# Packed attention and SwiGLU on one core: float32 second products in the first two units, GpSimd in place of a copy by DMA, and a new set of planner constants

## The chip, the core and the metric

The kernel runs on one core of a Trainium2 chip. The metric is device time in microseconds; lower is better. Three runs of the kernel before took 787.19, 790.18 and 791.77 us (median 790.18).

## The reference, cut to what matters

```python
def sm_attn(qq, kk, vv):                      # per batch and head
    s = scale * qq @ kk.T
    a = exp(s - max(s)); a = a / (sum(a) + 1e-9)
    return a @ vv
packed = sm_attn(p, k, v)                     # 32 packed rows read 576 keys
out    = sm_attn(q, packed, packed)           # 576 queries read the 32 packed rows
x = out as [4608 tokens, 512]                 # 8 batches x 576, 8 heads x 64
xn = x / sqrt(mean(x*x) + 1e-6) * rms_g
y = (silu(xn @ w_gate) * (xn @ w_val)) @ w_out     # 512 -> 1536 -> 512
```

The inputs q, k, v and p are float32. The three weight matrices arrive as float64, 1 MB for each of 18 pieces, and are made into float32 on the chip.

## The kernel before

The 4608 tokens are 12 units of 384 tokens, three tiles of 128 tokens each. A batch has 576 tokens, so units 1, 4, 7 and 10 hold tokens of two batches ("mixed" units). For each of the 8 batches `keysets` loads and transposes the keys, `stage1` makes the packed rows (32 per head), and `packed_weights` multiplies the packed rows by the gate and value weights (L1203) into a `ring` of eight slots: instead of forming x and multiplying it by the weights, the MLP multiplies the attention weights by these products. For each unit `query` brings the queries, `attention` makes the scores (L1405 or L1412), the softmax, the transposed weights `aT` and from them the second product (L1475), which is only needed for the RMS norm: ScalarE squares and sums it (L1483). The scaled weights, transposed again, are `aTu`. `mlp` then runs 24 groups of six matmuls per unit (L1593, two for each of 12 feature tiles `ft`), `gated` turns two of them into `hall` (silu L1644, product L1647, a high float16 part L1664 or L1667, a low part L1670 or L1673), and three groups of 36 matmuls (L1629, "second MLP products") make 128 output rows each, which `store` evicts.

Most products are made from float16 high and low parts, three matmuls for one. Batches and units below `EARLY = 2` take another way: their scores are float32 matmuls and their transposes go through TensorE (`transposed`, L1280) instead of a DMA. Their second product is before made like all others, of three float16 parts: `transposed` writes the high part by ScalarE (L1305) and the low part by VectorE (L1307), and `stage1` splits the packed rows `pk` into `pav` (L1163, by `split`, L452 and L454).

The weights: `gv_piece` (12 pieces of w_gate and w_val) and `wo_piece` (6 pieces of w_out) load float64 into a raw room and call `to_f32`, which uses ScalarE (L487), then GpSimd (L492) and VectorE (L494), or VectorE alone (L497, L499), as the letters of `LOW` and `LOW_WO` say. The raw rooms lie in tiles that are not in use yet: rooms 0 to 3 in `ring`, 4 to 6 in `wo`, 7 and 8 in `hall`. `RAW_AT` and `WO_AT` give each piece its room; a piece waits until the piece before it in its room is converted, loads are issued in turn, and in unit 0 the writes to `hall` wait for room 7 (`ft` up to 5) and room 8 (`ft` from 5 on). After each value piece `gv_piece` makes three scale columns `gv_sc` by four VectorE steps of one element per partition (L599, L600, L601, L607). When all six w_out pieces are there, `wo_scale` makes one scale from them, and `wo_split` writes each piece's high part by ScalarE into a spare tile (L687), its low part by VectorE in place (L689), and copies the high part to its place in `wo` by a DMA on SyncE's queue (L691). The second MLP products of unit 0 wait for these pieces, two `ft` each.

The order of all this is fixed when the kernel is built. Each function is a generator that yields steps (engine, estimated cost), and `Plan.run` plays them through a model of the engines and writes the instructions in that order into each engine's queue; the engines then run their queues in order and wait for semaphores. `RANK` and `LATER` say which chain goes first, `CHOICE` how far past the earliest possible start (in estimated us) a step of better rank may still be taken first on an engine, separately for stage 0 (until unit 1's `aTu` is planned) and stage 1, and `SLACK` adds 0.317 or 0.223 us to the start of a TensorE step that is not the MLP's. `Plan.fill` puts short matmuls of no use (L1717) into long planned gaps of TensorE.

```python
            window = CHOICE[self.stage][e]
            chain = min(
                (s for s in starts if ENGINE[s[2].ask[0]] == e and s[0] <= first[0] + window), key=lambda s: (s[1], s[0])
            )[2]
```

## Time and profile before

| | |
|---|---|
| median of three runs | 790.18 us |
| the profiled execution | 790.56 us, its span 788.4 us |
| TensorE busy (matmuls) | 748.3 us, 95% of the span |
| VectorE, ScalarE, GpSimd busy | 495.6, 465.3, 46.8 us |
| mean granted TensorE clock | 0.985 |

The span runs from the first to the last instruction; the profiled execution's own time is 2.2 us longer. A profile line gives an engine (PE is TensorE's matmuls, PEld its weight loads, DVE VectorE, ACT ScalarE, POOL GpSimd, SPq SyncE's queue of DMAs), a source line of the kernel, the tile written and the tiles read, and times. The chain of waits follows the work that ended last back from the end; in it "issue" is time in which the engine waited for nothing that the profile shows.

### The profile page before, as it was taken

The page shows a single profiled execution, that of the slowest core. Times are in us where ns is not written, and L with a number is a line of the kernel's source. Part 1 is how long each engine was busy: PE and PEld are TensorE (multiplying, and loading weights), DVE is VectorE, ACT ScalarE, POOL GpSimd, SP SyncE. Part 2 cuts the span into 40 slices and gives each one's busy share as a digit, 9 for nine tenths or more (in the row PEclk, how much of TensorE's full clock was granted, in tenths as well). Part 3 has the DMA queues.
Part 4 walks back from the last instruction along what each step waited for, and adds up shares of the span by engine and source line. Part 5 has one row for each costly group of instructions (what it writes and reads, how often), then busy time and mean ns, then how long its engine had stood idle before and what let it go on. Part 6 is the DMA issues. An engine that isn't in the chain of part 4 may idle for free.

```text
span 788.4 us, 18226 instructions
## 1 busy us (share of the span) xinstructions
PE 748.3 (95%) x7664; PEld 435.8 (55%) x7664; DVE 495.6 (63%) x1086; ACT 465.3 (59%) x884; POOL 46.8 (6%) x52
## 2 busy tenths in 40 slices
PE   8767997999999999999999999999999999999998
PEld 6533563676445555586455455586455455685553
DVE  1799986685496485568476674668476655472341
ACT  3778986576486576387377656287376455271230
POOL 1443101010000000000000000000000000000000
PEclk9989998999999999999999999999999999999999
DMA  9999234444637636714843470614613212301001
GB/s 254 387 300 250 113 94 109 90 88 109 125 78 136 138 64 132 150 43 79 170 98 65 102 157 8 151 42 91 157 36 60 69 35 61 90 13 34 27 1 41
DMA packets 137138, 83.76 MB, mean 106 GB/s; under 512 B 98528, under 2 KB 124640, under 8 KB 137056
## 3 DMA queue, kind: packets, MB, share of 16 engines
q1 hardware_dynamic: 137056, 82.59, 43.7%
q8 instruction: 60, 0.98, 0.5%
q14 instruction: 22, 0.18, 0.1%
HBM read 47.97 MB, written 9.44 MB: 73 GB/s over the span
## 4 chain that ended last, share of the span: by engine, by line
PE 72%; DVE 7%; ACT 5%; issue 3%; DMA 2%; SPq 0%; DVEq 0%; ACTq 0%
PE pm_2x L1629 9%; PE pm_1x L1629 9%; PE pm_0x L1629 9%; PE pm_0x L1593 8%; PE pm_2x L1593 7%; PE pm_1x L1593 7%; PE pm_3x L1629 6%; PE pm_3x L1593 6%; PE pm_3x L1203 1%; PE quad L1412 1%; PE quad L1052 1%; DVE ring L454 1%; PE pm_2x L1203 1%; PE quad L1475 1%; DVE t_0x L1647 1%
## 5 line engine op out<-in xcount | busy, mean ns | idle before, releaser
L1593 PEld LDWEIGHTS <-ring 128*128 128x128 f16 x2304 | 206.2, 98 | 106.9 <-issue 36.1
L1629 PEld LDWEIGHTS <-hall 128*128 128x128 f16 x1296 | 124.3, 99 | 157.1 <-issue 18.0
L1629 PE MATMUL pm_1x<-wo,hall 128*128 128x512 f16 x396 | 90.2, 382 | 0.0
L1629 PE MATMUL pm_2x<-wo,hall 128*128 128x512 f16 x324 | 73.9, 379 | 0.7 <-issue 0.7
L1629 PE MATMUL pm_0x<-wo,hall 128*128 128x512 f16 x324 | 73.4, 379 | 0.0
L1667 ACT CAST hall<-t_1x 128x384 f16<-128x384 f32 x72 | 36.8, 511 | 42.3 <-DVE t_1x L1647 42.2
L1667 ACT CAST hall<-t_0x 128x384 f16<-128x384 f32 x70 | 35.7, 510 | 36.5 <-DVE t_0x L1647 35.8
L1629 PE MATMUL pm_3x<-wo,hall 128*128 128x512 f16 x252 | 57.2, 382 | 0.0
L1673 DVE TENSOR_TENSOR hall<-t_1x,hall 128x384 f16<-128x384 f32 x70 | 38.9, 556 | 20.6 <-ACT hall L1667 19.1
L1593 PE MATMUL pm_0x<-aTu_0x,ring 128*128 128x192 f16 (+1 forms) x360 | 50.4, 283 | 1.5 <-ACT t_1x L1644 1.0
L1673 DVE TENSOR_TENSOR hall<-t_0x,hall 128x384 f16<-128x384 f32 x67 | 37.1, 554 | 16.7 <-ACT hall L1667 16.3
L1593 PE MATMUL pm_2x<-aTu_1x,ring 128*128 128x192 f16 (+1 forms) x300 | 43.3, 288 | 0.5 <-ACT t_0x L1644 0.4
L1593 PE MATMUL pm_0x<-aTu_1x,ring 128*128 128x192 f16 (+1 forms) x300 | 42.7, 286 | 0.4 <-DVE t_0x L1647 0.2
L1593 PE MATMUL pm_1x<-aTu_1x,ring 128*128 128x192 f16 (+1 forms) x300 | 42.4, 284 | 0.7 <-ACT t_0x L1644 0.7
L1593 PE MATMUL pm_1x<-aTu_0x,ring 128*128 128x384 f16 (+1 forms) x264 | 40.1, 293 | 0.5 <-DVE ring L454 0.2
L1593 PE MATMUL pm_2x<-aTu_0x,ring 128*128 128x192 f16 (+1 forms) x288 | 40.1, 283 | 0.0
L1593 PE MATMUL pm_3x<-aTu_1x,ring 128*128 128x384 f16 (+1 forms) x252 | 38.4, 294 | 1.5 <-issue 1.5
L1593 PE MATMUL pm_3x<-aTu_0x,ring 128*128 128x384 f16 (+1 forms) x240 | 35.3, 291 | 0.3 <-DVE ring L454 0.3
L454 DVE SCALAR_TENSOR_TENSOR ring<-pm_3x,pw_sc,ring 128x512 f16<-128x512 f32 x31 | 23.1, 744 | 3.8 <-ACT ring L452 3.7
L1483 ACT ACTIVATE quad<-quad 128x512 f32<-128x512 f32 x36 | 21.0, 584 | 6.0 <-PE quad L1475 5.8
L452 ACT ACTIVATE ring<-pm_3x,pw_sc 128x512 f16<-128x512 f32 x31 | 21.1, 681 | 4.6 <-PE pm_1x L1203 4.0
L454 DVE SCALAR_TENSOR_TENSOR ring<-pm_1x,pw_sc,ring 128x512 f16<-128x512 f32 x24 | 17.9, 747 | 7.4 <-ACT ring L452 7.0
(868 smaller groups left out, 1246.4 us busy)
## 6 DMA issues: line engine op xcount, KB each, us to landing
out_dram<-o_0x SPq DMA_DIRECT2D x18, 256.0 KB, 2.1
out_dram<-o_1x SPq DMA_DIRECT2D x18, 256.0 KB, 2.0
hall<-in_moe_w_out_dram SPq DMA_DIRECT2D x4, 1024.0 KB, 8.4
big_3x<-in_k_dram SPq DMA_DIRECT2D x7, 576.0 KB, 6.3
big_4x<-in_k_dram SPq DMA_DIRECT2D x6, 576.0 KB, 6.4
big_3x<-in_v_dram SPq DMA_DIRECT2D x6, 576.0 KB, 5.7
wo<-in_moe_w_gate_dram SPq DMA_DIRECT2D x3, 1024.0 KB, 15.2
wo<-in_moe_w_val_dram SPq DMA_DIRECT2D x3, 1024.0 KB, 13.0
```

What stands on the lines that cost most here:

```text
L452: nc.scalar.activation(hi, x, AF.Copy, scale=s)
L454: nc.vector.scalar_tensor_tensor(lo, x, s, hi, ALU.mult, ALU.subtract)
L1052: nc.tensor.matmul(pp[32 * j : 32 * j + 32, :D], a1T[:, c, 32 * j : 32 * j + 32], vf[:, j, cv, :], start=(c == 0), stop=(c == NCK - 1),)
L1203: nc.tensor.matmul(ps[e][32 * j : 32 * j + 32, :], pg[h, j, :], wgv[h, c, j, :, :].rearrange("p w f -> p (w f)"), start=True, stop=True,)
L1412: nc.tensor.matmul(ps2[o : o + n, i, :, pi, :], qT[:, lq, i, pi, o : o + n], packs[b][3][:, lp, pi, :, :], start=(j == 0), stop=(j == 2),)
L1475: nc.tensor.matmul(px[o : o + n, j, i, g, :], aT[h, i, la, g, o : o + n], packs[b][2][g][h, lp, :], start=(n3 == 0), stop=(n3 == 2), tile_ ...
L1483: nc.scalar.activation(x, x, AF.Square, scale=2.0**-14, accum_out=ss[:, i : i + 1])
L1593: nc.tensor.matmul(psi[:, :, o : o + n], pw[:, g, lw, w, f * P : (f + 1) * P], aT[:, :, la, g, o : o + n], start=(j == 0), stop=(j == 5),)
L1629: nc.tensor.matmul(po, hall[:, ft, lh, ts], wo[:, ft, 1 - lw, :], start=(n == 0), stop=(n == 3 * NFT - 1))
L1647: nc.vector.scalar_tensor_tensor(hall32[:, ft, :] if full else t, pss[1][:, :UT], sc[:, c, 2:3] if full else sc[:, c, 1:2], t, ALU.mult, A ...
L1667: nc.scalar.copy(hall[:, ft, 0, :], t)
L1673: nc.vector.tensor_tensor(hall[:, ft, 1, :], t, hall[:, ft, 0, :], ALU.subtract)
```

## The change

In units 0 and 1 the second product is made by float32 matmuls, one where there were three: `transposed` with `whole=True` writes `aT` as float32, two thirds by ScalarE and one third by VectorE, the packed rows are read as they are from `pks`, their scale `sv` goes into the square (`svs`, `svu`), batch 0's `pav` parts are no longer made, the unit waits for "normed" instead of "packed", and the four `pk` rooms are kept until unit 1's second product. The high parts of w_out go to their place by GpSimd (`WO_HI`, one of six by ScalarE) instead of a DMA. Three of the four `gv_sc` steps move from VectorE to GpSimd and the fourth is gone. Constants change: `WO_AT` (the raw rooms of w_out), letters that move single steps between engines, the planner's ranks, windows, latencies and step costs. `PW32` and `H32` stay off, and `PW16_FROM` stays at 8, so that all eight batches multiply by float32 weights.

```diff
--- before.py
+++ after.py
@@ -31,13 +31,13 @@
     mybir.EngineType.SP,
 )
-LATENCY = {PE: 0.299, ACT: 0.16, EXP: 0.16, SILU: 0.16, DVE: 0.14, POOL: 0.006}
+LATENCY = {PE: 0.299, ACT: 0.16, EXP: 0.16, SILU: 0.16, DVE: 0.14, POOL: 0.005}
 SLACK = (0.317, 0.223)
-CHOICE = ({'pe': 0.0, 'act': 0.458, 'dve': 0.275, 'pool': 0.298, 'sp': 0.833}, {'pe': 0.0, 'act': 0.382, 'dve': 0.13, 'pool': 0.269, 'sp': 0.274})
+CHOICE = ({'pe': 0.1, 'act': 0.458, 'dve': 0.275, 'pool': 0.298, 'sp': 0.833}, {'pe': 0.2, 'act': 0.382, 'dve': 0.13, 'pool': 0.2, 'sp': 0.274})
 IN_TURN = range(18)
 FILL = (0.9, 1.0, 400.0, 0.6)
@@ -56,8 +56,8 @@
-ACT_COST = (0.081, 0.87e-3)
-DVE_COST = (0.068, 0.953e-3)
+ACT_COST = (0.093, 0.87e-3)
+DVE_COST = (0.074, 0.953e-3)
 def act(n):
@@ -234,19 +234,19 @@
-RANK = ({"mlp": 1e9, "scales": 0, "gated": 0, "pw_evict": 0.63, "store": 0, "attention": 0.16, "stage1": 0.84, "keys": 0.18, "v": 0, "query": 0.3, "pw": 0.44, "g": 1.01, "w": 1.45, "wo": 1.05, "wo_split": 1.49, "conv": 2.38}, ...
-LATER = {"attention": -0.78, "stage1": -0.4, "keys": 0.45, "query": 0.4, "pw": -0.46, "w": 0.34, "wo": 0.0, "wo_split": 0.02}
+RANK = ({"mlp": 1e9, "scales": 0, "gated": 0.24, "pw_evict": 0.63, "store": 0, "attention": 0, "stage1": 0.84, "keys": 0, "v": 0, "query": 0.61, "pw": 0.44, "g": 0.77, "w": 1.34, "wo": 1.05, "wo_split": 1.49, "conv": 2.38}, ...
+LATER = {"attention": -0.92, "stage1": -0.4, "keys": 0.45, "query": 0.4, "pw": -0.46, "w": 0.34, "wo": 0.0, "wo_split": 0.02}
 RAW_AT = (0, 1, 2, 3, 4, 5, 6, 7, 8, 4, 5, 6)
-WO_AT = (7, 3, 8, 7, 3, 8)
+WO_AT = (8, 3, 7, 8, 3, 8)
 EARLY_ROOMS = (5, 4, 3)
 KT_IN_W = Q0_IN_W = True
 A1_ROOMS = 2
 A1T_BY = "AAAADAAA"
 VAL_BY = "DDPADD"
-LOW = "PPPPPPPPPPPP"
+LOW = "PPPPPPPPPDPP"
 LOW_WO = "PPPDDP"
 NORM_BY = "AAGAAAAAAAAA"
@@ -254,14 +254,14 @@
 KEYS_AFTER = 12
 KEYS_BY = "ADAAAAADAADA"
 QUERY_BY = "AADADA"
-H_HI = "AAAADAAAAADA"
-H_LO = "DDDPPDDDDDDP"
-H_LO_MIXED = "DDDDPDDDDDDD"
+H_HI = "AAAADAAAADDA"
+H_LO = "DPDDPDDDDDPP"
+H_LO_MIXED = "DDDDDDDDDDDD"
 H_LO_ONE = "DDDDDDDDDDDD"
-NORM_SLACK = (1.152, 3.0)
+NORM_SLACK = (1.416, 1.977)
 PW16_FROM = 8
@@ -274,10 +274,14 @@
 H32 = False
 PW32 = False
-PW_BY = "ADADADADADAD"
+PW_BY = "ADADADADDDAD"
 A1D_FROM = 8
 A1S_BY = "PPPPPPPPPPPPPPPP"
+GV_BY = "PPPPPP"
+WO_HI = "PPAPPP"
 @with_exitstack
@@ -361,7 +365,8 @@
     wo = wo32.bitcast(F16).rearrange("p f (l n) -> p f l n", l=2)
-    gv_sc = cpool.tile([P, NFC, 3], F32, name="gv_sc")
+    NSC = 3 if H32 else 2
+    gv_sc = cpool.tile([P, NFC, NSC], F32, name="gv_sc")
     pw_sc = cpool.tile([P, NFC], F32, name="pw_sc")
     wo_sc = cpool.tile([P, NFC], F32, name="wo_sc")
     wo_ss = cpool.tile([P, NFC], F32, name="wo_ss")
@@ -412,7 +417,7 @@
     rooms("tiny", 96, [P, 2], F32)
     rooms("trio", 8, [P, 3], F32)
     rooms("t24", 4, [P, 24], F32)
-    rooms("usc", 2, [P, NFC, 3], F32)
+    rooms("usc", 2, [P, NFC, NSC], F32)
     rooms("ru2", 2, [P, TPU], F32)
     if PW32:
@@ -595,16 +600,13 @@
             yield POOL, 2.9
             nc.gpsimd.tensor_scalar_mul(x, x, mx[:, 0:1])
         plan.mark("pw_sc", c)
-        yield DVE, 0.5, t0
-        nc.vector.tensor_scalar(gv_sc[:, c, 0:1], u[:, 0:1], gmax, 2.0**-5, ALU.mult, ALU.mult)
-        nc.vector.tensor_scalar(gv_sc[:, c, 1:2], s[:, 0:1], gmax_r, 2.0**-12, ALU.mult, ALU.mult)
-        nc.vector.tensor_scalar(wo_sc[:, c : c + 1], u[:, 0:1], u[:, 1:2], gsq, ALU.mult, ALU.mult)
+        by = nc.gpsimd if GV_BY[c] == "P" else nc.vector
+        yield POOL if GV_BY[c] == "P" else DVE, 0.6, t0
+        by.tensor_scalar(gv_sc[:, c, 0:1], u[:, 0:1], gmax, 2.0**-5, ALU.mult, ALU.mult)
+        by.tensor_scalar(gv_sc[:, c, 1:2], s[:, 0:1], gmax_r, 2.0**-12, ALU.mult, ALU.mult)
+        by.tensor_scalar(wo_sc[:, c : c + 1], u[:, 0:1], u[:, 1:2], gsq, ALU.mult, ALU.mult)
         if H32:
-            nc.vector.tensor_scalar(
-                gv_sc[:, c, 2:3], gv_sc[:, c, 1:2], wo_sc[:, c : c + 1], 2.0**-8, ALU.mult, ALU.mult
-            )
-        else:
-            nc.vector.tensor_copy(gv_sc[:, c, 2:3], gv_sc[:, c, 1:2])
+            by.tensor_scalar(gv_sc[:, c, 2:3], gv_sc[:, c, 1:2], wo_sc[:, c : c + 1], 2.0**-8, ALU.mult, ALU.mult)
         plan.mark("gv_sc", c)
         if PW32:
             plan.mark("sc", 0, c)
@@ -687,8 +689,12 @@
         nc.scalar.activation(hi, x, AF.Copy, scale=sc)
         yield DVE, dve(1024)
         nc.vector.scalar_tensor_tensor(wo[:, 2 * i : 2 * i + 2, 0, :], x, sc, hi, ALU.mult, ALU.subtract)
-        yield LOAD, P * 2048
-        nc.sync.dma_start(wo[:, 2 * i : 2 * i + 2, 1, :], hi)
+        if WO_HI[i] == "P":
+            yield POOL, 1.2
+            nc.gpsimd.tensor_copy(wo[:, 2 * i : 2 * i + 2, 1, :], hi)
+        else:
+            yield ACT, act(1024)
+            nc.scalar.copy(wo[:, 2 * i : 2 * i + 2, 1, :], hi)
         plan.give("o", hi0)
         plan.mark("wo_hl", i)
@@ -1110,13 +1116,14 @@
         for g in range(2):
             nc.tensor.matmul(pn, ones, ss[:, g : g + 1], start=(g == 0), stop=(g == 1))
         yield DVE, 0.8
-        uv, sv, eps = uvs[b], tiny(), epss[b]
+        uv, sv, eps = uvs[b], svs[b] if early else tiny(), epss[b]
         norm_scale(uv, sv, pn)
         if early:
...
         yield DVE, 0.2
         nc.vector.tensor_scalar(eps, sv, sv, 1e-6 * 2.0**-20, ALU.mult, ALU.mult)
+        plan.mark("normed", b)
         if not early:
             yield ACT, act(128), max(t_s, t_t)
             nc.scalar.activation(pts, ptx, AF.Copy, scale=sv)
@@ -1153,19 +1160,21 @@
             yield from split(pg[:, 0], pg[:, 1], pg32, 1.0, 128)
             plan.give("pg", pg32)
         pav = []
-        packs[b] = (uv, eps, pav, pbd, pg)
+        packs[b] = (uv, eps, pav, pbd, pg, pks)
         plan.mark("pg", b)
         plan.now = t_b
         plan.mark("pb", b)
-        for g in range(2):
+        for g in range(2) if (b + 1) * S > EARLY * UT else ():
             hl = yield Room("pav")
             yield from split(hl[:, 0], hl[:, 1], pks[g], sv, D, t_s)
-            plan.give("pk", pks[g])
+            if not early:
+                plan.give("pk", pks[g])
             pav.append(hl)
         plan.mark("packed", b)
     uvs = [cpool.tile([P, 1], F32, name=f"uv{b}") for b in range(B)]
+    svs = [cpool.tile([P, 1], F32, name=f"sv{b}") for b in range(EARLY)]
     epss = [cpool.tile([P, 1], F32, name=f"eps{b}") for b in range(B)]
@@ -1270,7 +1279,7 @@
         n = min(P, (S - r) // TPU)
         return [(b, r, 0, n)] + ([(b + 1, 0, n, P - n)] if n < P else [])
-    def transposed(dst, x, s, give, u=None):
+    def transposed(dst, x, s, give, u=None, whole=False):
         psc = yield Room("psc")
         ps = psc.rearrange("p a b -> p (a b)")[:, : TPU * HR]
@@ -1283,15 +1292,15 @@
         if give:
             plan.give("e", x)
         ps = ps.rearrange("p (i x) -> p i x", i=TPU)
-        if PW32 and u == 0:
-            x = whole(dst)
+        if whole or PW32 and u == 0:
+            x = whole32(dst)
             t0, ends = plan.now, []
             yield ACT, act(512), t0
-            nc.scalar.activation(x[:, :2], ps[:, :2].rearrange("p i (g t) -> p i g t", g=2), AF.Copy, scale=2.0)
+            nc.scalar.activation(x[:, :2], ps[:, :2].rearrange("p i (g t) -> p i g t", g=2), AF.Copy, scale=s)
             ends.append(plan.now)
             yield DVE, dve(256), t0
-            nc.vector.tensor_scalar_mul(x[:, 2], ps[:, 2].rearrange("p (g t) -> p g t", g=2), 2.0)
+            nc.vector.tensor_scalar_mul(x[:, 2], ps[:, 2].rearrange("p (g t) -> p g t", g=2), s)
             plan.now = max(ends + [plan.now])
             plan.give("psc", psc)
             return
@@ -1307,7 +1316,7 @@
         nc.vector.scalar_tensor_tensor(lo, ps, s, hi, ALU.mult, ALU.subtract)
         plan.give("psc", psc)
-    def whole(aT):
+    def whole32(aT):
         return aT.rearrange("p i l g t -> p (i l g t)").bitcast(F32).rearrange("p (i g t) -> p i g t", i=TPU, g=2)
@@ -1438,7 +1447,7 @@
             plan.give("t24", x)
         aT = yield Room("aT")
         if early:
-            yield from transposed(aT, e, 2.0**14, False)
+            yield from transposed(aT, e, 1.0, False, whole=True)
         else:
             ehl = yield Room("hl")
             yield ACT, act(768)
@@ -1453,11 +1462,16 @@
         t_a = plan.now
         for b, r, o, n in parts(u):
-            yield ("packed", b)
+            yield ("normed" if early else "packed", b)
+        svu = svs[parts(u)[0][0]] if early else None
         if len(parts(u)) > 1:
+            if early:
+                svu = tiny()
             yield DVE, 0.3
             for b, r, o, n in parts(u):
                 nc.vector.tensor_copy(eps[o : o + n], epss[b][o : o + n])
+                if early:
+                    nc.vector.tensor_copy(svu[o : o + n], svs[b][o : o + n])
         ss = trio()
         t_x = []
@@ -1468,6 +1482,15 @@
         yield PE, pe(D, 6 * TPU) + 0.4, t_a
         for i in range(TPU):
             for g in range(2):
+                if early:
+                    for j in range(4):
+                        h = slice(32 * j, 32 * j + 32)
+                        for b, r, o, n in parts(u):
+                            nc.tensor.matmul(
+                                px[o : o + n, j, i, g, :], whole32(aT)[h, i, g, o : o + n], packs[b][5][g][h, :],
+                                start=True, stop=True, tile_position=(32 * j, o),
+                            )
+                    continue
                 for n3, (la, lp) in enumerate(((0, 0), (0, 1), (1, 0))):
                     for j in range(4):
                         h = slice(32 * j, 32 * j + 32)
@@ -1480,11 +1503,15 @@
         for i in range(TPU):
             yield ACT, act(512) + 0.2, t
             x = px[:, :, i].rearrange("s j g d -> s j (g d)")
-            nc.scalar.activation(x, x, AF.Square, scale=2.0**-14, accum_out=ss[:, i : i + 1])
+            nc.scalar.activation(x, x, AF.Square, scale=svu if early else 2.0**-14, accum_out=ss[:, i : i + 1])
             t_x.append(plan.now)
         for name, room in held:
             plan.give(name, room)
         plan.give("aT", aT)
+        if u == EARLY - 1:
+            for b in range(EARLY):
+                for x in packs[b][5]:
+                    plan.give("pk", x)
         if u * UT // S != (u + 1) * UT // S:
             b = u * UT // S
@@ -1536,7 +1563,7 @@
             yield ACT, 3 * act(256), t_r
             for i in range(TPU):
                 nc.scalar.activation(e[:, i], e[:, i], AF.Copy, scale=rr[:, i : i + 1])
-            yield from transposed(aTu, e, 1.0, True, u)
+            yield from transposed(aTu, e, 2.0 if PW32 and u == 0 else 1.0, True, u)
         else:
             ahl = yield Room("hl")
             for i in range(TPU):
@@ -1580,7 +1607,7 @@
                         pw = ring[:, slot_of(b, c)]
                         if PW32 and b == 0:
                             pw = pw.rearrange("p e l w f -> p e (l w f)").bitcast(F32)
-                            x = aths[0] if u else whole(aT)
+                            x = aths[0] if u else whole32(aT)
                             for g in range(2):
                                 nc.tensor.matmul(
                                     psi[:, :, o : o + n], pw[:, g, 2 * P * w + f * P : 2 * P * w + (f + 1) * P], x[:, :, g, :],
```

More of the change, by code (lines that the diff above doesn't have):

```diff
@@ L233, in run @@
             self.go(chain)
-RANK = ({"mlp": 1e9, "scales": 0, "gated": 0, "pw_evict": 0.63, "store": 0, "attention": 0.16, "stage1": 0.84, "keys": 0.18, "v": 0, "query": 0.3, "pw": 0.44, "g": 1.01, "w": 1.45, "wo": 1.05, "wo_split": 1.49, "conv": 2.38}, {"mlp": 1e9, "scales": 0.03, "gated": 0, "pw_evict": 0, "store": 0.25, "attention": 1.21, "stage1": 0.58, "keys": 0.27, "v": 0.78, "query": 0.42, "pw": 1.83, "g": 2.14, "w": 0.92, "wo": 2.54, "wo_split": 0.63, "conv": 2.76})
-LATER = {"attention": -0.78, "stage1": -0.4, "keys": 0.45, "query": 0.4, "pw": -0.46, "w": 0.34, "wo": 0.0, "wo_split": 0.02}
+RANK = ({"mlp": 1e9, "scales": 0, "gated": 0.24, "pw_evict": 0.63, "store": 0, "attention": 0, "stage1": 0.84, "keys": 0, "v": 0, "query": 0.61, "pw": 0.44, "g": 0.77, "w": 1.34, "wo": 1.05, "wo_split": 1.49, "conv": 2.38}, {"mlp": 1e9, "scales": 0.03, "gated": 0, "pw_evict": 0, "store": 0.25, "attention": 1.21, "stage1": 0.58, "keys": 0.27, "v": 0.78, "query": 0.42, "pw": 1.83, "g": 2.14, "w": 0.92, "wo": 2.54, "wo_split": 0.63, "conv": 2.76})
+LATER = {"attention": -0.92, "stage1": -0.4, "keys": 0.45, "query": 0.4, "pw": -0.46, "w": 0.34, "wo": 0.0, "wo_split": 0.02}
 RAW_AT = (0, 1, 2, 3, 4, 5, 6, 7, 8, 4, 5, 6)
-WO_AT = (7, 3, 8, 7, 3, 8)
+WO_AT = (8, 3, 7, 8, 3, 8)
 EARLY_ROOMS = (5, 4, 3)
```

## The prediction, made before the result was known

> **What bounds the kernel now.** I read the page first, then busy time by stretch (columns: length, then busy us and instruction counts of PE, PEld, DVE, ACT and POOL, PEclk, DMA share, GB/s), then the chain of waits from 124 us on.
>
> ```profile
> span 788.4 us, 18226 instructions
> PE 748.3 (95%) x7664; PEld 435.8 (55%) x7664; DVE 495.6 (63%) x1086; ACT 465.3 (59%) x884; POOL 46.8 (6%) x52
> q8 instruction: 60, 0.98, 0.5%
> ```
> ```profile
> 60.00:73.00 13.00, 8.09 (x83) 4.25 (x77) 12.59 (x35) 12.30 (x20) 5.35 (x5) 0.98 1.05 278
> 73.00:90.20 17.20, 14.71 (x123) 8.10 (x123) 16.26 (x35) 15.36 (x29) 1.75 (x2) 0.91 0.53 194
> 90.20:104.50 14.30, 13.57 (x131) 8.64 (x130) 11.45 (x27) 13.44 (x23) 1.83 (x2) 1.00 0.03 9
> 154.30:788.40 634.10, 621.67 (x6285) 359.95 (x6282) 382.26 (x828) 355.42 (x697) 13.78 (x14) 1.00 0.39 83
> ```
>
> From 154 us on TensorE is busy for 621.67 of 634.10 us and the change takes nothing out of that work. What can move the end is therefore how early the stretch begins, and the pauses in it. From 60 to 90 us VectorE is the full engine (12.59 of 13.00, 16.26 of 17.20), ScalarE nearly so, and TensorE waits: 2.49 us idle in the second row, and it also runs fillers there. The one large hole later is in the chain:
>
> ```profile
> 123.89 0.65 PE pm_3x L1629 x3
> 124.54 0.54 PE pm_0x L1203
> 125.56 1.40 PE pm_3x L1629 x6
> 126.96 1.29 PE quad L1475 x143
> 128.25 3.77 issue
> 132.02 0.21 PE quad L1475
> 132.23 1.39 PE pm_3x L1629 x3
> 133.62 0.99 PE pm_2x L1203
> 135.51 2.99 PE pm_1x L1629 x9
> ```
> ```profile
> 130.60:134.00 3.40, 1.98 (x12) 0.51 (x19) 0.34 (x1) 1.67 (x5) 0.00 (x0) 0.50 0.02 5
> 134.00:137.40 3.40, 3.40 (x21) 0.72 (x6) 2.05 (x8) 2.50 (x6) 0.86 (x1) 0.50 0.21 77
> ```
>
> 143 of unit 1's 144 second-product matmuls run in 1.29 us, then TensorE stands for 3.77 us with one to go, waiting for no semaphore. Within the pause the DMA view of 128.25 to 132.02 has one packet of the instruction queue:
>
> ```profile
> q8 instruction: 1, 0.02, 1.9%
> ```
>
> The page has 60 such packets for 7664 matmuls and as many weight loads: 15328/60 = 255 instructions each, so they are TensorE's code. The burst of 144 pairs is 288 instructions, more than a packet, in 1.3 us. I read the pause as TensorE out of code. Afterwards the granted clock is 0.50 until 137.4, and the same work takes longer: three matmuls of L1629 1.39 instead of 0.65 (0.74 lost), a block of L1203 1.89 (133.62 to 135.51) instead of 1.02 (124.54 to 125.56; 0.87 lost), nine of L1629 2.99 instead of 3 x 0.65 = 1.95 (1.04 lost). The burst costs 3.77 + 2.65 = 6.42 us.
>
> **The change part by part.**
>
> *Second products in float32.* A float32 matmul is two instructions: L1405 of unit 1 issues 24 in the code and 48 stand in the trace.
>
> ```profile
> 91.37 0.81 PE quad L1052 x48
> 113.37 1.80 PE quad L1405 x48
> ```
>
> So unit 1's burst goes from 144 pairs to 96, 192 instructions, less than a packet, and unit 0's from 72 to 48. Time on TensorE: 96 passes of 64 columns, bounded by the rates of these two rows, 2 x 0.81 = 1.62 and 2 x 1.80 = 3.60 us, less what four row groups side by side save (the 144 float16 ones take 1.29, or 0.86 for 96). I take 1.3, no difference, between -0.4 and +2.3. The pause and its half clock should go: -6.42 us. If a packet's end still fell at the start of the burst, some 64 further instructions would have to run before the next end; at L1593's rate of six pairs in 0.97 us (row below) that is 5 us, as long as the pause's own wait for code (126.96 to 132.02). So the pause mostly goes wherever the end falls.
>
> The code of all later bursts shifts by 24 + 48 pairs, 144 instructions, 0.56 of a packet. The later mixed units keep their 144 pairs:
>
> ```profile
> 312.87 3.34 PE pm_1x L1629 x15
> ```
> ```profile
> 487.14 1.30 PE quad L1475 x144
> 489.84 0.69 issue
> ```
> ```profile
> 634.74 0.97 PE pm_0x L1593 x6
> 635.71 1.30 PE quad L1475 x144
> 637.28 1.49 issue
> 638.77 1.45 PE pm_3x L1593 x5
> 640.22 1.92 PE pm_2x L1593 x6
> ```
>
> Unit 4's burst ends at 312.87 with no pause, unit 7's is followed by 0.69, unit 10's by 1.49 and eleven slow matmuls (3.37 instead of 11 x 0.162 = 1.78, 1.59 lost): 3.77 together. Half a packet's shift takes a packet's end away from those two and may bring it to unit 4. I take both as gone and one of half their sum as new: -1.9, between -3.8 (none) and 0 (as many as now).
>
> *VectorE's relief.* In the timeline of VectorE:
>
> ```profile
> 82.73 0.20 DVE L599 TENSOR_SCALAR gv_sc<-tiny_37x,gmax 128x1 f32<-128x1 f32 x1
> 83.15 0.14 DVE L607 COPY gv_sc<-gv_sc 128x1 f32<-128x1 f32 x1
> 124.12 0.28 DVE L454 SCALAR_TENSOR_TENSOR pav_3x<-pk_3x,tiny_47x,pav_3x 128x64 f16<-128x64 f32 x1
> 124.95 0.95 DVE L1307 SCALAR_TENSOR_TENSOR aT_0x<-quad,aT_0x 128x768 f16<-128x768 f32 x1
> 83.42 0.69 DVE L497 TENSOR_SCALAR wo<-wo 128x1024 uint32<-128x1024 uint32 x1
> ```
>
> The four gv_sc steps take 82.73 to 83.29, 0.56 us, six times: 3.4. Of L1307 a third stays, about 0.4, twice: 1.1 saved. Batch 0's two pav parts: 0.56. Against that, LOW's ninth letter gives VectorE one more step like L497: 0.7. The other letters swap single steps of about half a us and cancel. Relief 4.3 us. ScalarE gains under 1 us (two pav parts, a smaller aT, one copy more of w_out); I cost it at nothing, since VectorE covers it; without that cover it is that 1 us.
>
> GpSimd gets 18 steps of one column and five copies of 128x1024. It has room (5.35 busy of 13.00 us), but it gets in VectorE's way:
>
> ```profile
> 68.14 0.17 DVE L440 TENSOR_SCALAR tiny_29x<-tiny_29x 128x2 f32<-128x2 f32 x1
> 68.34 1.02 DVE L441 TENSOR_SCALAR tiny_30x<-tiny_29x 128x2 uint32<-128x2 uint32 x1
> ```
> ```profile
> 68.23 1.10 POOL L492 TENSOR_SCALAR ring<-ring 128x1024 uint32<-128x1024 uint8 x1 [4.29 <-DMA ring<-in_moe_w_out_dram]
> ```
>
> A step of 0.17 takes 1.02 while GpSimd runs L492, 0.85 longer. Not every meeting does this. The price of 11 new meetings (six groups, five copies) is between 0 and 11 x 0.85 = 9.4 us; I take a third of them at 0.85, about 2.8. What stays is 4.3 - 2.8 = 1.5 us, and as VectorE is full from 60 to 90 us I carry it to the end whole: -1.5. Bounds: TensorE cannot gain more there than its gaps, 2.49 us of idle and the longest run of fillers,
>
> ```profile
> 83.17 1.80 PE L1717 MATMUL quad<-fill,onesb 128*128 128x256 bf16 x15
> ```
>
> 4.29 together, and at the other end it may lose 4.3 - 9.4 = -5.1. The Trainium skill, SBUF — State Buffer, section "Who interferes with whom", speaks against the change here: a VectorE step with two SBUF inputs, or in a two-port mode, and a GpSimd step shut each other out for a whole instruction; L441 agrees. If each of the five copies held VectorE for its whole length as there, 5.5 us, the relief would turn into -1.2, and the sum below would be 2.7 us more.
>
> *The copy instead of the DMA.* The DMA view gives
>
> ```profile
> wo<-o_0x SPq DMA_DIRECT2D x3, 256.0 KB, 2.5
> ```
>
> 2.5 us to landing; the copy I put at L492's 1.10 us (as many elements), bounded by 0.85 less and by as much more if VectorE holds it up. Each piece is ready about 1.4 us sooner. The second products of unit 0 start at 117 us with pieces made long before and meet only the last two late; until then other groups fill TensorE. I cost it at nothing; without that cover it would be one such difference, 1.4 us. SyncE's queue loses six issues, nothing waits behind them.
>
> *Rooms and waits.* With WO_AT the last w_out load waits for the fourth one's conversion instead of the third's, so it is issued later; it also frees room 7 for unit 0's first `hall` writes earlier. The two work against each other, and I take 0. Keeping the four pk rooms until unit 1's second product holds up batch 2's packed rows alone, whose keys are loaded only about then. Units 0 and 1 wait for "normed", which comes before "packed". In stage 1, TensorE's window goes from 0 to 0.2 us: below.
>
> *Sum.* 790.56 - 6.42 - 1.9 - 1.5 = 780.7 us. The profiled execution is 0.05% above the median of 790.18, so no correction is made.
>
> **The rivals.**
>
> *More comes of it.* All late pauses go (-3.77) and the gaps between 73 and 90 us close whole (-4.29): 790.56 - 6.42 - 3.77 - 4.29 = 776.1. For it: VectorE is at its limit just there. Against: ScalarE is at 15.36 of 17.20 as well, and it is hardly relieved.
>
> *The pause stays, or its like comes back elsewhere.* Then only the relief is left: 790.56 - 1.5 = 789.1. For it: 192 instructions still nearly empty a packet, and DMA traffic delays the fetch. The Trainium skill's page Runtime: NRT & Kernel Launch, section "Instruction fetch mechanics", holds the crossing of a block to be mostly hidden; by it the pause is something else than code, would have no reason to go, and the time would be about this 789.1. The packet inside the pause speaks against it.
>
> *TensorE's queue is held up in stage 1 (slower).* With a window of 0.2 us a step of another chain may be put ahead of the MLP's matmuls up to 0.2 us before its planned start. About 120 such steps follow (nine for each of six batches, 36 packed-weight groups, three for each of ten units). If its data are then late, the queue stands, with the MLP behind it. At the full 0.2 us that is 24 us; at a mean of 0.12 us it is 14.4, and the time 780.7 + 14.4 = 795.1. It decides from (794.1 - 780.7)/120 = 0.11 us each. Against: the planned start holds 0.223 us of slack already, and the last row by stretch shows only 12.4 us of gaps in 634 with every pause in it, so data are mostly there early.
>
> **How the numbers follow.** A measurement of this kernel can tell about 0.5%, 3.95 us, from no change: faster is below 786.2, slower above 794.1. Forecast 0.5, more 0.2, the pause stays 0.2, the queue 0.1. Faster 0.5 + 0.2 = 0.7, same 0.2, slower 0.1. The range goes from 776.1, less the 0.73 us of idle in 90.2 to 104.5, = 775.3, to 789.1, plus some 0.5 us of a dearer float32 product, = 789.6; it leaves out the slower case and the edges of the others.
>
> **What would show it right or wrong.** Right: L1475 of unit 1 in 96 float32 matmuls, no "issue" of over 1 us behind it, clock 1.00 from 90 us to past 300; TensorE's end of unit 0 some 1 to 2 us earlier, DVE below 16.26 in a stretch like 73 to 90; pauses behind units 4, 7 and 10 that add up to less than 2.2 us. Wrong: the pause still behind unit 1's burst, at a burst with no code packet in it (then it was not code); VectorE steps near the w_out copies stretched by a whole us each; gaps in front of L1412, L1475 or L918 after 150 us that sum to many us.

## The result and the profile after

The changed kernel took 782.89 us (median of five runs, 781.70 to 783.64) against 790.18 before: ratio 0.9906, 95% interval 0.988 to 0.9933. That is 7.3 us faster, where the sum would have it 9.5 below the same median. The profiled execution took 781.70 us.

The head, the engines and the instruction queue on the page of after:

```profile
span 779.9 us, 18069 instructions
PE 742.9 (95%) x7591; PEld 435.2 (56%) x7591; DVE 491.8 (63%) x1067; ACT 467.0 (60%) x882; POOL 56.5 (7%) x71
q8 instruction: 59, 0.97, 0.5%
```

The chain of waits of after at unit 1's burst, and at unit 4's:

```profile
127.03 1.18 PE quad L1489 x72
128.21 0.75 PE pm_0x L1656 x3
...
303.27 1.26 PE quad L1498 x139
304.53 2.01 issue
```

Unit 1's 48 float32 matmuls, 96 in the trace's count (of which the chain shows x72), take 1.18 us with no pause behind them; three matmuls of L1656 take 0.75 there, not 1.39. The pause has not left the kernel, though: 139 pairs into unit 4's burst TensorE stands for 2.01 us, as it did before at unit 1, with no half clock afterwards (1.00 in both rows, same columns as in the prediction's windows):

```profile
303.20:306.60 3.40, 1.39 (x145) 1.27 (x144) 0.00 (x0) 0.00 (x0) 0.00 (x0) 1.00 0.31 86
306.60:310.00 3.40, 3.40 (x21) 1.59 (x21) 0.00 (x0) 3.09 (x9) 0.00 (x0) 1.00 0.03 5
```

The early stretches of after:

```profile
60.00:73.00 13.00, 10.32 (x78) 6.07 (x78) 11.26 (x30) 11.05 (x20) 7.56 (x11) 0.74 1.07 295
73.00:90.20 17.20, 13.64 (x124) 8.35 (x131) 16.04 (x29) 17.17 (x30) 3.52 (x6) 1.00 0.62 216
```

VectorE falls from 12.59 to 11.26 and from 16.26 to 16.04, but ScalarE is now full (17.17 of 17.20), and nothing is won up to the burst: it starts at 127.03, before at 126.96. The whole 8.5 us of span between these two executions come after that.

### The profile page after: what moved, and what is told of

Same layout as the page of the kernel before. It is cut to its first block, busy times and chain, and to the rows that moved or that the text cites. A ratio compares the mean times of both kernels' runs of the same rounds, so it can differ in the third digit from the quotient of the medians.

```text
span 779.9 us, 18069 instructions
## 1 busy us (share of the span) xinstructions
PE 742.9 (95%) x7591; PEld 435.2 (56%) x7591; DVE 491.8 (63%) x1067; ACT 467.0 (60%) x882; POOL 56.5 (7%) x71
## 4 chain that ended last, share of the span: by engine, by line
PE 75%; ACT 7%; DVE 7%; DMA 5%; issue 3%; SPq 1%; POOL 1%; ACTq 0%; DVEq 0%; POOLq 0%
PE pm_3x L1620 8%; PE pm_1x L1656 8%; PE pm_1x L1620 8%; PE pm_2x L1656 8%; PE pm_3x L1656 8%; PE pm_0x L1620 8%; PE pm_0x L1656 7%; PE pm_2x L1620 6%; PE pm_0x L1212 2%; DMA ring<-in_moe_w_gate_dram 2%; PE quad L1421 1%; PE quad L1058 1%; PE pm_2x L1212 1%; DMA aT_0x<-hl_0x 1%; PE quad L1498 1%
## 5 line engine op out<-in xcount | busy, mean ns | idle before, releaser
L1656 PEld LDWEIGHTS <-hall 128*128 128x128 f16 x1296 | 123.7, 98 | 149.5 <-issue 10.9
L1656 PE MATMUL pm_2x<-wo,hall 128*128 128x512 f16 x360 | 82.2, 379 | 0.0
L1656 PE MATMUL pm_1x<-wo,hall 128*128 128x512 f16 x360 | 81.7, 379 | 0.0
L1656 PE MATMUL pm_3x<-wo,hall 128*128 128x512 f16 x324 | 73.2, 379 | 0.0
L1656 PE MATMUL pm_0x<-wo,hall 128*128 128x512 f16 x252 | 58.1, 379 | 0.0
L1620 PE MATMUL pm_3x<-aTu_1x,ring 128*128 128x192 f16 (+1 forms) x342 | 48.1, 284 | 0.4 <-ACT t_0x L1671 0.4
L1620 PE MATMUL pm_3x<-aTu_0x,ring 128*128 128x384 f16 (+1 forms) x300 | 44.6, 291 | 3.8 <-DVE ring L459 1.5
L1620 PE MATMUL pm_0x<-aTu_0x,ring 128*128 128x192 f16 (+1 forms) x264 | 36.7, 283 | 1.3 <-DVE ring L459 0.9
L1620 PE MATMUL pm_2x<-aTu_1x,ring 128*128 128x384 f16 (+1 forms) x210 | 32.0, 294 | 0.0
L459 DVE SCALAR_TENSOR_TENSOR ring<-pm_0x,pw_sc,ring 128x512 f16<-128x512 f32 x28 | 20.9, 747 | 6.8 <-ACT ring L457 6.5
L459 DVE SCALAR_TENSOR_TENSOR ring<-pm_2x,pw_sc,ring 128x512 f16<-128x512 f32 x26 | 19.4, 745 | 6.0 <-ACT ring L457 5.8
```

The source lines that it names most:

```text
L459: nc.vector.scalar_tensor_tensor(lo, x, s, hi, ALU.mult, ALU.subtract)
L1620: nc.tensor.matmul(psi[:, :, o : o + n], pw[:, g, lw, w, f * P : (f + 1) * P], aT[:, :, la, g, o : o + n], start=(j == 0), stop=(j == 5),)
L1656: nc.tensor.matmul(po, hall[:, ft, lh, ts], wo[:, ft, 1 - lw, :], start=(n == 0), stop=(n == 3 * NFT - 1))
```

## The experiments

Every run of an experiment stood beside runs of the kernel before on the same chip, whose medians were 789.45, 789.67 and 789.09 us in the three groups below (790.18 beside the changed kernel), so times of different groups are compared to about 1 us at best. Four questions: is the pause code, what are the float32 products worth alone, what are GpSimd's steps worth, and what does the new order cost? "Kept order" means that the planner's steps stay as they are and only what a step issues is changed, so that every engine has its work in the order of the base kernel.

### Parts taken out of the source, and a shift of code

**e1**, before, with half as many fillers of twice the width (122 instructions less):

```diff
-        for _ in range(n):
+        m = min(n // 2, self.merges)    # merges: no limit here
+        self.merges -= m
+        for _ in range(m):
+            matmul(spare[0][1], 2)      # 512 columns
+        for _ in range(n - 2 * m):
             matmul(spare[0][1])
```

> The kernel before, in which the fillers (L1717) are half as many and twice as wide: 61 pairs of weight load and matmul fewer, all ahead of unit 1's second product, so that TensorE's code moves by 122 instructions against the 256 of a code packet; nothing of the change is in it. Theory (the place of a packet's end in a burst of 288 instructions makes the pause): no pause over 1 us behind the bursts of units 1, 4, 7 and 10 and no half clock after 90 us, 790.2 - 6.4 - 3.8 = about 780. First rival (only the shorter float32 burst takes the pause away): the pause behind unit 1 stays, 790. Second rival (the relief of VectorE, the copies and the planner's constants make the gain): 790.

Measured: 783.59 us (780.35 to 785.84), ratio 0.9917 (0.9892 to 0.9943). The chain of waits at unit 1:

```profile
127.16 1.30 PE quad L1480 x144
128.46 0.75 PE pm_3x L1634 x3
```

All 144 pairs in one piece, no pause, full clock; the time is 3.6 us above the 780 expected, and why is not known. A shift of code that computes nothing gives about what the whole change gives. That the pause is code is shown by this; that the change's gain is this pause is not yet.

**e2**, before with the float32 products alone, as the diff has them, with the constants of before:

```diff
-            yield from transposed(aT, e, 2.0**14, False)
+            yield from transposed(aT, e, 1.0, False, whole=True)
...
-            plan.give("pk", pks[g])
+            if not early:
+                plan.give("pk", pks[g])
```

> The kernel before with the float32 second products of units 0 and 1 alone; constants, copies and scale columns as before. Theory: unit 1's burst has 192 instructions, and the later bursts lie with a packet's end well inside them, so no pause over 1 us: about 780 to 782. First rival: the same. Second rival (relief, copies, constants): 789 to 790.

Measured: 828.0 us (824.97 to 832.02), ratio 1.0488 (1.0461 to 1.0515): wrong by far. The waits of TensorE from 190 to 380 us (total, times, longest):

```profile
PE pm_1x L1614 <- DMA aTu_0x<-hl_0x: 11.0, 1, 11.0
PE pm_3x L1614 <- DVE tiny_19x L1428: 4.8, 1, 4.8
PE pm_3x L1614 <- DVE tiny_88x L1428: 4.3, 1, 4.3
```

With two more of 2.7 us for packed rows these are 25.5 us of waits for steps that come late, which neither the kernel before nor the changed one has. The planner gives other steps other places as soon as a step changes its cost, its wait or its room, and it found a bad order here. So this run says nothing of float32 matmuls.

**e3**, the whole change without the float32 products, and **e4**, the same with 66 pairs of its fillers merged:

```diff
-            yield from transposed(aT, e, 1.0, False, whole=True)
+            yield from transposed(aT, e, 2.0**14, False)
```

> The whole change without the float32 second products (float16 parts, as before). By the counted code the packets' ends fall 155, 82, 62 and 166 instructions into the bursts of units 1, 4, 7 and 10, and pauses were seen only where one fell 24 to 44 instructions in. Theory: no pause over 1 us, although unit 1's burst has its 288 instructions again: 780 to 782, no slower than the kernel after. First rival (the float32 burst is what takes the pause away): the pause is back, 782.9 + 6.4 = about 789. Second rival: 783, as the kernel after.

> The same kernel as the one with the whole change but the float32 products, with 66 filler pairs fewer (fillers twice as wide), which puts a packet's end 32 instructions into unit 1's burst and 42 into unit 10's, as in the kernel before (31 and 34). Theory: the pause of 3 to 4 us behind unit 1 is back with a half clock, and one of 1 to 1.5 us behind unit 10: 786 to 790, some 6 to 8 us more than without the shift. First rival (the length alone): pauses with and without the shift, no difference between the two. Second rival: as the kernel after, 783, no difference either.

Measured: e3 790.31 us (788.53 to 794.17), ratio 1.001 (0.9994 to 1.0027); e4 794.72 us (793.28 to 795.46), ratio 1.0062 (1.0043 to 1.0081). The chains of waits, e3 first:

```profile
137.37 0.74 PE quad L1481 x76
138.11 1.31 issue
```
```profile
140.75 1.29 PE quad L1486 x142
142.04 2.76 issue
```

e3's burst starts at 137.37, 10.3 us later than after's, and this execution's span ends 10.1 us later: net, all of its loss lies ahead of the burst, in an order that was planned anew once more. So its time, near the first rival's 789, does not speak for that rival. But the theory missed too: it had no pause over 1 us with a packet's end 155 instructions into the burst, and there is one of 1.31 us, with half clock behind it (granted clock 0.50 from 140.47 to 143.88). The shift moves the pause from the middle of the burst to its end and makes it 1.45 us longer, without half clock; e4 is 4.4 us slower than e3, where 6 to 8 were expected, and its burst starts 3.4 us later, so that the pause is not what most of this is. What these two say of the parts is spoilt by the order, as in e2. From here on the order was held.

### The order kept: the products, the small steps, the burst's length

**e5**, before in its kept order, with float32 second products:

```diff
+            if early:
+                nc.scalar.activation(pav32[b][:, g], pks[g], AF.Copy, scale=sv)
...
+                            nc.tensor.matmul(
+                                px[o : o + n, j, i, g, :], whole(aT)[h, i, g, o : o + n], pav32[b][h, g, :],
+                                start=True, stop=True, tile_position=(32 * j, o),
+                            )
```

> The kernel before, every step in its planned place, with the second products of units 0 and 1 in float32: the steps are planned as before, and only what they issue is changed (float32 aT by thirds on ScalarE and VectorE, float32 packed rows in a tile of their own, 24 or 48 float32 matmuls in place of 72 or 144). Theory (the products are sound, and the 828 us of the run with the float32 part alone come from the order that the planner made of it): no waits after 200 us beyond those of before, unit 1's pause and its half clock gone (-6.4), the pauses of units 7 and 10 gone (-3.8) and one of 2 to 4 us new at unit 4, where a packet's end falls 23 instructions into the burst: about 782, 780 to 785. Rival (float32 matmuls are slow or hold something up by themselves): 800 or more.

Measured: 782.42 us (780.49 to 784.91), ratio 0.9909 (0.989 to 0.9929), as expected. None of e2's waits is there, and unit 1 has no pause; unit 4 has the new one, shorter than the 2 to 4 us expected (chain of waits):

```profile
126.25 1.18 PE quad L1491 x72
127.43 0.75 PE pm_3x L1654 x3
...
304.80 1.26 PE quad L1500 x139
306.06 1.15 issue
```

So the products alone, in the old order, are worth 789.67 - 782.42 = 7.25 us, and e2's 828 us are the order. Which of e2's edits makes the planner's order bad (the held `pk` rooms, the wait for "normed", the step costs) wasn't tried.

**e6**, after in its kept order, with GpSimd's steps undone:

```diff
-        by = nc.gpsimd if GV_BY[c] == "P" else nc.vector
+        by = nc.vector
...
-            nc.gpsimd.tensor_copy(wo[:, 2 * i : 2 * i + 2, 1, :], hi)
+            nc.sync.dma_start(wo[:, 2 * i : 2 * i + 2, 1, :], hi)
```

> The changed kernel, every step in its planned place, with the gv_sc steps issued on VectorE and the five w_out copies issued as DMAs again. Theory (GpSimd's part of the change is worth little): within 1 us of the changed kernel, 782 to 784. Rival (VectorE's relief is real and carried to the end): 785 or more, with TensorE's second MLP products of unit 0 starting 1 to 3 us later. Third possibility, GpSimd's steps cost more than they save: under 781.

Measured: 786.20 us (785.37 to 787.45), ratio 0.9957 (0.994 to 0.9974). The rival holds: the small steps are worth 3.3 us in the change's order. Who waited for the tile `gv_sc` in e6 (us, times):

```profile
  ACT usc_0x L1586: 2.2, 2
```

That is ScalarE, which scales it. In e6's chain of waits VectorE has one step behind the other from 59 to 71 us, `gv_sc` last, and then comes ScalarE:

```profile
70.57 0.20 DVE gv_sc L605
71.13 1.12 ACT wo L492
...
130.07 1.18 PE quad L1489 x72
```

Unit 1's burst starts 3.04 us later than in after (130.07 against 127.03), one execution of each.

**e7**, after with nine fillers split in two (18 instructions more ahead of unit 1), and **e8**, the same with half of unit 1's burst issued twice:

```diff
+        for _ in range(2 * m):          # m up to 9 in all
+            matmul(spare[0][1], 0)      # 128 columns each
...
+        if u == 1:
+            for i, g in ((2, 0), (2, 1), (2, 0)):
+                for j in range(4):
...
+                        nc.tensor.matmul(
+                            px[o : o + n, j, i, g, :], whole32(aT)[h, i, g, o : o + n], packs[b][5][g][h, :],
```

> The changed kernel with nine of its fillers split in two (18 instructions more, all before unit 1): a packet's end now falls 32 instructions into unit 1's burst, where it fell before the change, and 7 instead of 25 instructions into unit 4's. The burst itself stays at 192 instructions. Theory (it takes a burst longer than a packet): no pause at unit 1, unit 4's pause of 2.0 us gone or smaller, 779.5 to 782. Rival (the place of the packet's end alone decides): a pause of 2 to 4 us with half clock at unit 1, 785 to 788.

> The same as the run before it, with half of unit 1's float32 burst issued a second time into the same places (288 instructions instead of 192, results unchanged, about 0.6 us of TensorE more). A packet's end falls 32 instructions into it, and none near the start of the later bursts. Theory: a pause of 2 to 4 us near the end of the burst and half clock behind it, 4 to 7 us more than the run with the short burst: 785 to 788. Rival (float32 bursts do not run out of code, or the pause has another cause than length and place): 0.6 us more only, 780 to 783.

Measured: e7 781.21 us (780.86 to 782.82), ratio 0.9895 (0.9877 to 0.9912); e8 780.01 us (779.51 to 782.02), ratio 0.9882 (0.9862 to 0.9902). The chain of waits of e7, then e8:

```profile
126.98 1.18 PE quad L1494 x72
128.16 0.75 PE pm_0x L1661 x3
```
```profile
127.61 0.53 PE quad L1512 x29
128.14 1.14 issue
129.27 0.27 PE quad L1512
129.54 0.75 PE pm_0x L1670 x3
```

192 instructions run through with a packet's end at the place that had the pause before; 288 float32 instructions at the same place pause. (e7's unit 4 still stands for 1.69 us, 130 pairs into its burst.) So it takes the length and the place, and float32 does not protect. But the pause is 1.14 us, not 2 to 4, and the clock stays full (three matmuls 0.75), so the 4 to 7 us did not come, and the time, 785 to 788 expected, is the rival's. e8 even ends lower, though within the intervals; its doubling moved the packets' ends away from unit 4's burst, which has no pause in it. What makes a pause long was still open.

### What makes the pause long, and the two routes in the old order

**e9**, before in its kept order, with the small steps on GpSimd (the reverse of e6's edit), and **e10**, before in its kept order with the edits of e5 and e9 and 22 pairs of fillers merged, so that no packet's end lies near the start of a long burst:

> The kernel before, every step in its planned place, with the gv_sc steps on GpSimd (three instead of four) and the six w_out copies on GpSimd instead of a DMA, nothing else. TensorE's code and so the places of the packets are those of before, and the pauses stay. Theory A (the small steps are worth about 3 us in any order, as the 3.3 us that undoing them cost in the changed kernel's order): about 786. Theory B (they are worth that only in an order that was planned with them on GpSimd): 789 to 790. Theory C (GpSimd's steps fall into VectorE's and cost): over 791.

> The kernel before, every step in its planned place, with the float32 products and the small steps on GpSimd as in the two runs that do each alone, and 22 pairs of fillers merged into wide ones so that no packet's end lies near the start of a long burst. Theory: the 782.4 of the float32 products in this order, less unit 4's pause of 1.15 and what half clock it brings, less 0 to 3.3 for the small steps: 777.5 to 781.3. Rival (the changed kernel's own order and constants are needed for its gain): 782 or more.

Measured: e9 786.00 us (783.24 to 788.57), ratio 0.9961 (0.9947 to 0.9975); e10 781.07 us (778.91 to 781.95), ratio 0.9888 (0.9871 to 0.9905). e9's 3.1 us look like theory A. The chain of waits says otherwise:

```profile
128.60 1.29 PE quad L1473 x143
129.90 1.01 issue
130.91 0.18 PE quad L1473
131.09 0.75 PE pm_3x L1627 x3
```

The burst starts 1.64 us later than before in this execution (128.60, not 126.96); what the edit wins is the pause, 1.01 instead of 3.77 us and no half clock, with TensorE's code at the same place. The pauses of units 7 and 10 stay (0.81 and 1.70 us). The DMA engines during the pause (40 slices of the window, tenths busy): before from 126.9 to 132.1, then e9 from 128.5 to 131:

```profile
DMA  9999999999999999964500000000000000000000
```
```profile
DMA  0900000000000000000000000000000000000000
```

Before, the loads of batch 2's keys fill the engines until 129.4, and the code packet (the 5, from 129.45 on) comes behind them; in e9 the engines are idle and the packet comes at once. SyncE's queue shows why, before first, then e9:

```profile
120.56 0.59 SPq L691 DMA_DIRECT2D wo<-o_1x  x1
121.20 2.02 SPq L720 DMA_DIRECT2D pf_0x<-in_p_dram  x4
123.32 0.38 SPq L702 DMA_DIRECT2D big_3x<-in_k_dram  x1
```
```profile
90.32 0.31 SPq L700 DMA_DIRECT2D big_3x<-in_k_dram  x1
```

The six copies of w_out stood in the queue ahead of the loads, each waiting for its data; without them the key load goes out at 90.32 instead of 123.32, 33 us earlier, and is over long before the burst.

e10 against e5 is 1.35 us less, with intervals that overlap, and unit 4's pause accounts for 1.15 of it: apart from pauses the small steps are worth nothing measurable in the old order. There the copies get in VectorE's way: a step of unit 1's softmax (L1434 before, L1432 in e9) takes 0.18 us before, in its timeline, and 0.89 in e9, beside a copy on GpSimd:

```profile
122.32 0.89 DVE L1432 TENSOR_SCALAR t_1x<-t_0x 128x24 f32<-128x24 f32 x1
```
```profile
122.15 1.03 POOL L689 COPY wo<-o_1x 128x1024 f16<-128x1024 f16 x1
```

**e11**, after in its kept order, with only the copies issued as DMAs (the second half of e6's edit), and **e12**, e5 with half of unit 1's burst issued twice and 24 fillers split, so that TensorE's code has the length of before:

> The changed kernel, every step in its planned place, with only the five w_out copies issued as DMAs again; the gv_sc steps stay on GpSimd. Undoing both cost 3.3 us. If VectorE's gv_sc steps are what was saved (as the prediction's sum has it): 782 to 783.5. If the DMA in place of the copy makes the second MLP products of unit 0 late: 785 to 786.5.

> The kernel before, every step in its planned place, with float32 second products, but unit 1's burst made as long again as before (half of it issued twice, results unchanged, 288 instructions) and 24 fillers split, so that TensorE's code has exactly the 15328 instructions of before and every packet's end the place that it had. About 0.6 us of TensorE more. Theory (the gain of the float32 products is code alone): unit 1's pause of 3 to 4 us with its half clock is back, the pauses of units 7 and 10 too, 788 to 791. Rival (the gain is VectorE's and ScalarE's smaller work, or float32 bursts do not run out of code): 782 to 785.

Measured: e11 783.19 us (781.28 to 783.42), ratio 0.9922 (0.9908 to 0.9935): the copies are worth 0.3 us in the changed kernel, nothing that can be told, and `gv_sc` about the other 3.0. e12 792.07 us (790.92 to 794.91), ratio 1.0045 (1.0028 to 1.0062). Its chain of waits and two windows:

```profile
131.28 3.12 issue
134.40 0.26 PE quad L1514
134.66 1.39 PE pm_3x L1668 x3
...
492.47 0.80 issue
...
640.02 1.90 issue
```
```profile
130.60:134.00 3.40, 0.68 (x62) 0.55 (x47) 1.06 (x2) 0.00 (x0) 0.00 (x0) 0.94 0.38 89
134.00:137.40 3.40, 3.00 (x20) 0.51 (x19) 1.24 (x4) 2.64 (x7) 0.00 (x0) 0.50 0.02 5
```

With float32 products and the old code length, unit 1's pause is back at 3.12 us with its half clock (0.50; three matmuls 1.39), and so are the pauses of units 7 and 10 (0.69 and 1.49 before, 0.80 and 1.90 here), and the time is 9.65 us above e5, a little over the 788 to 791 expected. e12 issues 24 split fillers and 0.6 us of matmuls more than e5; the rest is code. In the old order, what the float32 products win is code.

## Why the prediction was right, and where its sizes were off

**Unit 1's pause, -6.42: right.** The mechanism is shown from both sides, by e1 and e5 (gone) and e12 (back). The float32 burst takes 1.18 us, where I had taken 1.3. One statement behind it was too narrow: "the pause mostly goes wherever the end falls" holds for the short burst (e7), but the old burst would have lost it by a shift too (e1), and most of it through the loads that the copies no longer hold back (e9). Any one of three edits takes all or most of it, so their gains don't add: with the loads early, as in the changed kernel, even the long burst would stand for 1.14 us only (e8).

**Late pauses, -1.9: right.** Units 7 and 10 have none (unit 10's burst ends at 637.54, the next matmuls start there), unit 4 has one of 2.01: 3.77 - 2.01 = 1.76 less. Unit 7 in after:

```profile
479.44 1.30 PE quad L1498 x144
480.74 1.08 PE pm_2x L1620 x6
```

The half clock that I counted into the 3.77 did not come at unit 4.

**The small steps, -1.5: the term that was mis-sized, twice.** In the change's order they are worth 3.3 us (e6), nearly all from `gv_sc` (3.0, e11), more than forecast and inside the bounds; VectorE is the chain there. The collisions that I set against it exist (0.18 to 0.89 us). By the Trainium skill's SBUF — State Buffer, "Who interferes with whom", they are what a step in a two-port mode beside a GpSimd step should show, and this row agrees. But they don't decide: without the copies on GpSimd the time is the same (e11).

**What failed: the new order at nothing.** The sum carried VectorE's relief "to the end whole", on before's order, and priced the constants only as a rival on TensorE's queue. But e6 has the same products as e5 and the old small steps, and differs from it in order, constants and a few single steps: 786.20 - 782.42 = 3.8 us slower. Of this 0.9 is unit 4's longer pause (2.08 us in e6, 1.15 in e5). The rest lies ahead of unit 1's burst, as far as one execution of each can say: it starts at 130.07 in e6 and at 126.25 in e5. The `gv_sc` steps win 3.04 of it back, and so after's burst starts at 127.03, no sooner than before's 126.96; the 1 to 2 us that TensorE was to be earlier by the end of unit 0 did not come. Such starts are not sharp: e12, in e5's order with some fillers split, starts the burst at 129.57. So the 3.8 us rest on the medians, and which constant or which step's place makes them stays open. In one line, by medians: 789.67 - 7.25 (products) + 3.8 (order and constants) - 3.0 (`gv_sc`) - 0.3 (copies) = 782.9. I had -8.3 (both pause terms), 0 and -1.5: 1.1 too much, 3.8 left out, 1.8 too little. The last hides half of the second, which is luck, as the small steps' price was set without a thought of the order; what is left is the 2.2 us by which the forecast of 780.7 lies below 782.89.

**SyncE's queue: wrong.** "SyncE's queue loses six issues, nothing waits behind them": the loads of p and k waited behind them, the keys' first by 33 us (e9). It costs nothing in the changed kernel, where the short burst has no pause left to win; in the old order it is the copies' whole gain.

**The rivals.** More did not come of it: ScalarE, and no longer VectorE, is full from 73 to 90 us. The pause did not stay at unit 1, but its like came back at unit 4. The Trainium skill's rule that crossing a block is mostly hidden (Runtime: NRT & Kernel Launch, "Instruction fetch mechanics") fits nearly all of the 59 packets of after, but not the one at unit 4's burst, nor three of the 60 of before. TensorE's queue in stage 1 is not held up: from 150 to 300 us TensorE is busy for 146.94 us in after and 146.96 before.

No kernel of the study is shown to beat the changed one. The lowest, e8 (780.01) and e10 (781.07), have intervals that overlap with it, though both do without unit 4's pause. The changed kernel with its fillers shifted to clear that pause and nothing else wasn't run.

## What to carry to other kernels

Before crediting an edit with a gain, ask what it does to the code's length and to the order: shift the code by instructions of no use (e1), and try the edit with every step held in its place (e5); a part taken out of a planned kernel and planned anew (e2, e3) measures the planner. A pause with "issue" behind a burst of several hundred short instructions, and one packet of the instruction queue in it or just before it, is code, the more surely if TensorE goes on about 1.4 us after that packet's end: shorten the burst, shift it, or keep loads off the DMA engines just then. Of a removed DMA, count what stood behind it in its queue.

## What was not expected of the hardware

A packet's end at the same place of a burst of 288 instructions cost 3.77 us, with half clock behind it, while the 16 DMA engines were busy with loads (3.12 in e12), and 1.01 or 1.14 us at full clock while they were idle (e9, e8). Unit 4's pause is a third such pair: 2.01 us in after, behind loads that end at about 304.1, and 1.15 in e5 with idle engines.

The traces give each packet's start and length, and a pause ends by them. In all 17 pauses of TensorE after 100 us that are put down to "issue" and last 0.69 us or more, over all kernels here, it goes on 1.3 to 1.6 us after the packet's end: before, the packet lasts from 129.45 to 130.57 and TensorE goes on at 132.02; in e9 it lasts from 128.56 to 129.52, and TensorE goes on at 130.91. Loads put the packet off, but they are not needed: at unit 10 before it lasts from 636.45 to 637.36 with idle engines, and the pause is 1.49. In e3 it starts at 136.69, ahead of the burst, and ends at 137.99; TensorE goes on at 139.41.

Whether half clock follows does not go by the pause's length alone: 1.31 us in e3 and 1.49 at unit 10 before brought it, 2.01 at unit 4 after and 2.76 in e4 did not. The Trainium skill's TensorE: Matmul & The Clock Gate, in Part 1 on the clock gate, has activity counted in free-running windows of about 3.4 us; a pause that falls whole into one window would then differ from one that straddles two. The traces agree on the length: the half clock from 130.57 to 137.39 before is two such lengths, that of e3 one. On the place they do not settle it: counted in steps of 3.41 us from the clock's last change, unit 10's pause before lies whole in one window (635.74 to 639.15) and unit 4's in after lies across a border (305.43), but e11's pause at unit 4 has 1.89 of its 2.08 us in one window and brings no half clock.
